# Moving one DMA sum five slots ahead, one load in front of two others, and two folds, in a fused attention + gated FFN kernel

## The chip, the cores and the metric

One NeuronCore of one Trainium2 chip runs the kernel. The metric is device time in microseconds (us), the median of several executions; smaller is better. A measurement of the kernel before and after takes the same inputs: four batches of 6016 rows with 256 columns, and weights 256 x 1536, 256 x 1536 and 1536 x 256.

## What is computed

```python
def _attn_ref(q, k, v, tau):                       # q, k, v: (4, 6016, 256)
    qn = q / (np.linalg.norm(q, axis=1, keepdims=True) + 1e-06)
    kn = k / (np.linalg.norm(k, axis=1, keepdims=True) + 1e-06)
    s = kn.transpose(0, 2, 1) @ qn / tau           # 256 x 256 per batch
    s = s - s.max(-1, keepdims=True)
    a = np.exp(s)
    a /= a.sum(-1, keepdims=True) + 1e-09
    return (v @ a).astype(np.float32)

def _moe_ref(x, w_gate, w_val, w_out):             # x: the result above, 24064 x 256
    gate = 1.0 / (1.0 + np.exp(-(x @ w_gate)))
    val = x @ w_val
    return (gate * val @ w_out).astype(np.float32)
```

The scores of a batch need all rows of its q and k; after that each row of v is on its own. Since the attention matrix `a` is only 256 x 256, the kernel multiplies it into the two input weights once per batch (the tiles `gh`, named G and H) and then applies G and H to v directly.

## The kernel before, in words

**Tiling.** The 6016 rows of a batch are 47 tiles of 128 rows. Four tiles make a *chunk* of 512 rows (the last has three), so a batch has 12 chunks, numbered 0 to 11. The 1536 hidden columns are 12 blocks of 128. One chunk runs through 12 *slots*, one for each block f: `glu(b, ci, f)` issues two matmuls into `ps_gate`, two into `ps_val`, a tanh on ScalarE (ACT) into `g_sb` (L656) and, on VectorE (DVE), the product into `hT` (L657). `ps_gate` and `ps_val` have two buffers each, so TensorE (PE) may be at most two slots ahead of ACT and DVE.

**Stages.** I call the 144 slots of batch b *stage b* (0 to 3). In the slots of a stage other work is put beside `glu`: the output matmuls `ps_o` of the chunk before, with DVE sums of `hT` (L679, `a_sum`: in slots 1, 3, 4, 5, 6 of a chunk for the second half of the previous chunk and in slots 7 to 11 for the first half of its own, none in slots 0 and 2); the evacuation of these results, which is two ACT copies (L733 into `m_sb`, L740 into `out_sb`) and four GpSimd (POOL) additions (L734, L735 on `m_sb`; L750, L751 on `out_sb`) for each pair of rows tiles; the store, from SyncE's (SP's) queue; and, in stages 0 to 2, the scores of the *next* batch.

**The next batch's scores.** The next batch's q and k come in six groups g0 to g5 of eight row tiles (the last of seven), q and k together in one tile `qk_sb`. Group g belongs to a first slot s0 = first + int(g * step), where first is 16 in stage 0 and 0 in the others, and step is (96 - first) / 6: 13.33 or 16 slots. In fixed slots after s0 each group gets: squares on ACT (L293, slots 0, 3, 6, 9) into `sq` tiles (two buffers); two accumulating DMAs of these into `acc` from POOL's queue (L304, slots 5 and 11); sums and differences of the halves of q and k, `qs0` to `qs4`, for a seven-product form of the score matmuls. `qs0`, `qs2`, `qs3`, `qs4` are DVE instructions (L328, L336, L341). `qs1`, the sum of q's two halves, is made by DMA: `score_sums` with m = 1 copies one half (L332, slot 1), and `score_sum_q` adds the other (L346, slot 6) with an accumulating DMA, which has to wait until the copy has landed. Both are issued from POOL's queue. `qs1` has two buffers. The score matmuls `ps_s` are spread from slot s0 + 3 (stage 0: s0 + 5) to the same point of the next group; the last two of the seven products read `qs1`.

**After the last group**, around slot 98 (s0 = 8 * FC + 2 in the code), `acc` is folded from eight tiles to one on DVE (L311: `acc_fold` with steps (4,), then (2, 1), for w = 1, k, and w = 0, q), `norms_mm` sums the columns, and the softmax and the next G and H follow.

**What sets the order.** `side_work(b)` writes a list by hand: `at(slot, fn, ...)` appends a call to the slot. Each engine works its instructions strictly in the order in which these calls issue them; inside a slot `glu` comes first, then the output matmuls, then the listed calls in the order of their appending. POOL therefore holds one sequence of additions and of DMA issues: `load_v` (L156), `load_qk` (L144, k then q; in stage 0 at max(9, s0 - 14), later at s0 - 24), `acc_add`, the two `qs1` DMAs. An instruction of POOL that waits holds back all that stand behind it. SP's queue holds the transposes of v (L621, `transpose_v`, into `vT`) and the stores.

`load_v` of chunk ci + 2 stands in slot 0 of chunk ci; only for (b, ci) = (0, 0) it stands in slot 10, behind the k and q load of g0 in slot 9. The loop over chunks stands first in `side_work`, so in equal slots `load_v` precedes `load_qk`.

Of the kernel before, what the change touches and what calls it, by code (L numbers as in the profile page):

```python
# [53 lines left out]
def kernel(  # L54
# [31 lines left out]
    FC = DFF // P  # L86
# [41 lines left out]
    def mm(out, lhsT, rhs, start, stop, **kw):  # L128
        nc.tensor.matmul(out, lhsT=lhsT, rhs=rhs, start=start, stop=stop, **kw)  # L129
# [30 lines left out]
    t0, nt = groups0[0]  # L160
# [39 lines left out]
    for f0, nf in pieces:  # L200
        if f0 + nf == DFF:
            load_v(0, 1)
        for w, src in enumerate((moe_w_gate, moe_w_val)):
            nc.gpsimd.dma_start(
                out=w_sb[w][f0 // FG][:, :, ds(f0 % FG, nf)],
# [6 lines left out]
    for n in range(FC // TPC):  # L212
        w_f32[n] = f32pool.tile([P, TPC, C], FP32, tag="f32", name="w_f32")
        nc.gpsimd.dma_start(
            out=w_f32[n], in_=moe_w_out.rearrange("(t p) c -> p t c", p=P)[:, n * TPC : (n + 1) * TPC, :]
# [16 lines left out]
    st = {}  # L232
# [82 lines left out]
    def score_sums(b, t0, m, halves):  # L315
        tl = qk[b, t0]
        s = st[b]
        if m == 0:
            s["sums"] = []
        out = qspool.tile([P, 2 * TPC, P], BF16, tag=f"qs{m}", name=f"qs{m}", bufs=1 + (m == 1))  # L320
        s["sums"].append(out)
        n = halves[0][1]
        lo, hi = (slice(h * TPC, h * TPC + n) for h in range(2))
        tt = nc.vector.tensor_tensor
        if m == 0:

            o = out.rearrange("p (t c) n -> p t c n", c=2).rearrange("p t c n -> p t (c n)")
            tt(out=o[:, :n], in0=tl[:, 1, hi, :], in1=tl[:, 1, lo, :], op=ALU.subtract)  # L328
        elif m == 1:

            o = out.rearrange("p (t c) n -> p t c n", c=2).rearrange("p t c n -> p t (c n)")
            nc.gpsimd.dma_start(out=o[:, :n], in_=tl[:, 0, lo, :])  # L332
        elif m == 2:

            o = out.rearrange("p (w t) n -> p w t n", w=2)
            tt(out=o[:, :, :n], in0=tl[:, :, lo, :P], in1=tl[:, :, hi, P:], op=ALU.add)  # L336
        else:

            w, op = ((0, ALU.subtract), (1, ALU.add))[m - 3]
            for u0, r in [(0, 2 * TPC)] if n == TPC else halves:  # L340
                tt(out=out[:, u0 : u0 + r], in0=tl[:, w, u0 : u0 + r, :P], in1=tl[:, w, u0 : u0 + r, P:], op=op)  # L341

    def score_sum_q(b, t0, halves):
        n = halves[0][1]
        o = st[b]["sums"][1].rearrange("p (t c) n -> p t c n", c=2).rearrange("p t c n -> p t (c n)")
        nc.gpsimd.dma_start(out=o[:, :n], in_=qk[b, t0][:, 0, TPC : TPC + n, :], accum_op=ALU.add)  # L346

    def score_work(b, t0, halves):
        tl, s = qk[b, t0], st[b]
        n = halves[0][1]  # L350
        first, last = t0 == 0, n < TPC
        work = []

        def raw(w, half, c):
            return lambda u: tl[:, w, half * TPC + u, ds(c * P, P)]

        def split(m, c):
            return lambda u: s_tile[m][:, 2 * u + c, :]

        def block(m, h):  # L360
            return lambda u: s_tile[m][:, h * TPC + u, :]

        s_tile = s["sums"]

        products = (
            (0, 0, raw(0, 0, 0), split(0, 1), None),
            (0, 1, raw(0, 1, 1), split(0, 0), (raw(0, 1, 1), raw(1, 1, 0))),
            (1, 0, block(2, 0), block(2, 1), (raw(0, 1, 1), raw(1, 1, 1))),
            (1, 1, block(3, 1), block(4, 1), (block(3, 1), block(4, 1))),
            (1, 2, block(3, 0), block(4, 0), None),  # L370
            (0, 2, split(1, 1), raw(1, 0, 0), None),
            (0, 3, split(1, 0), raw(1, 1, 1), (raw(0, 1, 0), raw(1, 1, 1))),
        )

        def go(i, bank, region, lhsT, rhs, u, end):
            if first and region == 0 and u == 0:
                pl, tag = ((pss, "s"), (psm, "m"))[bank]
                s["bank", bank] = pl.tile([P, 4, P], FP32, tag=tag, name=f"ps_s{bank}")
            mm(
                s["bank", bank][:, region, :],  # L380
                lhsT(u),
                rhs(u),
                start=(first and region == 0 and u == 0),
                stop=(last and end),
                skip_group_check=True,
            )

        for i, (bank, region, a, w, alone) in enumerate(products):
            us = [(a, w, u) for u in range(n)]
            if last and alone is not None:  # L390
                us += [(*alone, u) for u in range(n, TPC)]
            for e, (a1, w1, u) in enumerate(us):
                work.append((i, go, (i, bank, region, a1, w1, u, e == len(us) - 1)))
        return work
# [271 lines left out]
    sums = {}  # L666
# [169 lines left out]
    for g, (t0, nt) in enumerate(groups0):  # L836
# [11 lines left out]
        while adds:  # L848
            w, last_sq = adds.pop()
# [46 lines left out]
    def queue_scores(b, t0, halves):  # L896
        score_queue.extend(score_work(b, t0, halves))
# [7 lines left out]
    def side_work(b):  # L905


        side = {}

        def at(slot, fn, *a):  # L910
            side.setdefault(divmod(slot, FC), []).append((fn, a))

        for ci in range(NCH):
            nb, nci = (b, ci + 1) if ci + 1 < NCH else (b + 1, 0)
            lb, lci = (b, ci + 2) if ci + 2 < NCH else (b + 1, ci + 2 - NCH)
            if nb < B:
                at(ci * FC + 2, transpose_v, nb, nci)
            if lb < B:
                at(ci * FC + (10 if (b, ci) == (0, 0) else 0), load_v, lb, lci)
            if (b, ci) == (0, 0):  # L920
                for i in range(FC // TPC):
                    at(8, copy_w_out, i)
                for n, m in enumerate((1, 0, 3, 2, 4)):
                    for i in range(FC // TPC):
                        at(11 + 2 * n, sum_w_out, m, i)
        n = b + 1
        if n == B:
            return side
        first, last = (16 if b == 0 else 0), 8 * FC
        wide = [(t, min(2 * TPC, NT - t)) for t in range(0, NT, 2 * TPC)]  # L930
        step = (last - first) / len(wide)
        at(first - 1 if b == 0 else 0, acc_start, n)
        for g, (t0, nt) in enumerate(wide):
            s0 = first + int(g * step)
            halves = [(0, nt - TPC), (TPC, TPC)]
            if b == 0:
                at(max(FC - 3, s0 - 14), load_qk, n, t0, nt)
            elif s0 >= 24:
                at(s0 - 24, load_qk, n, t0, nt)
            for i in range(4):  # L940
                at(s0 + 3 * i, acc_square, n, t0, 1 - i // 2, halves, i % 2)
            for w in range(2):
                at(s0 + 11 - 6 * w, acc_add, n, t0, w, halves)
            late = 5 if b == 0 else 3
            for m, slot in enumerate((0, 1, 3, 6, 8 if b == 0 else 9)):
                at(s0 + slot, score_sums, n, t0, m, halves)
            at(s0 + 6, score_sum_q, n, t0, halves)
            end = first + int((g + 1) * step) + late
            at(s0 + late, queue_scores, n, t0, halves)
            for slot in range(s0 + late, end):  # L950
                at(slot, run_scores, s0 + late, end, slot)
        if n + 1 < B:
            for g, (t0, nt) in enumerate(wide[:2]):
                at(NCH * FC - 24 + 16 * g, load_qk, n + 1, t0, nt)
        s0 = 8 * FC + 2
        at(s0 - 3, acc_fold, n, 1, (4,))
        at(s0 - 2, acc_fold, n, 1, (2, 1))
        at(s0 + 1 if b == 0 else s0, acc_fold, n, 0, (4,))
        at(s0 + 2, acc_fold, n, 0, (2, 1))
        at(s0 + 5, score_out, n, 0)  # L960
        at(s0 + 6, norms_mm, n)
        at(s0 + 7, score_out, n, 1)
        at(s0 + 7, root_seed, n)
        at(s0 + 7, root_steps, n)
        at(s0 + 12, norms_inv, n)
        at(s0 + 12, spread_both, n)
        at(s0 + 14, read_row, n)
        at(s0 + 14, score_blocks, n)
        at(s0 + 22, scale_x, n, 0)
        at(s0 + 24, scale_x, n, 1)  # L970
        at(s0 + 25, exps, n, 0)
        at(s0 + 26, exps, n, 1)
        at(s0 + 28, all_sums, n)
        at(s0 + 28, gh_tiles, n)
        for i, piece in enumerate(gh_order):
            slot = s0 + 29 + 2 * i
            if slot < NCH * FC:
                at(slot, gh, n, piece, *((pss, "s"), (psm, "m"))[i % 2])
            else:
                spill.setdefault((n, *divmod(slot - NCH * FC, FC)), []).append((gh, (n, piece, psm, "m")))  # L980
        return side
# [73 lines left out]
```

## Time and profile before

| | |
|---|---|
| seven executions, median | 806.27 us |
| lowest and highest | 803.38 and 808.51 us |
| the profiled execution | 803.38 us, of which its span is 801.3 us |
| PE busy | 778.8 us of the span |
| granted PE clock over the span | 0.998 |
| DMA moved | 103.30 MB, 129 GB/s over the span |

The span runs from the first to the last instruction. Stage 0 begins at 37 us, after the first batch's scores; stages 1, 2 and 3 begin near 231, 423 and 615 us. A 512-column matmul pair starts 0.43 us before what follows it when nothing stalls, and a slot lasts 1.36 us where scores are made and 1.25 us where they are not.

How full the DMA engines are differs much between stages, and that is read from the page's second part, 40 slices of 20 us:

```profile
DMA  9999999962687999862578699877224223323302
GB/s 214 202 199 172 189 172 210 197 120 53 132 133 139 174 181 202 163 119 54 115 137 146 126 181 178 178 136 139 62 59 92 61 54 82 78 54 81 72 28 73
```

Each digit is the busy share of a slice in tenths. From 0 to 160 us, and around 260 to 320 and 460 to 520 us, the engines are nearly always busy; in stage 3 they are not. Where they are busy a transfer waits for those issued before it.

### The profile page before, as it was taken

What the parts mean: (1) busy time and instruction counts of PE and PEld (TensorE: products, weight loads), DVE (VectorE), ACT (ScalarE), POOL (GpSimd) and SP (SyncE); (2) the same over time, 40 slices, a digit from 0 to 9 for tenths busy, and PEclk for the clock granted to TensorE, in tenths of its full rate; (3) what the DMA queues carried; (4) which work ended last, traced back from release to release, by engine and by line L of the source; (5) the groups of instructions that cost most, each with busy time, mean ns of one, the idle gap of its engine ahead of it and who ended that gap; (6) DMA issues with size and microseconds to landing.
All of it is one profiled execution on the core that took longest, in us unless ns stands there. A gap on an engine that the chain in (4) does not pass through costs nothing.

```text
span 801.3 us, 18409 instructions
## 1 busy us (share of the span) xinstructions
PE 778.8 (97%) x6946; PEld 497.7 (62%) x6946; DVE 717.7 (90%) x1234; ACT 526.2 (66%) x893; POOL 416.8 (52%) x640
## 2 busy tenths in 40 slices
PE   3899999999999999999999999999999999999997
PEld 2556666666666666666666666666666566666666
DVE  5778999999979999999988999999998898998995
ACT  3766777766667667676667777666666566566563
POOL 3565667548443566565743564655744244444433
PEclk9999999999999999999999999999999999999999
DMA  9999999962687999862578699877224223323302
GB/s 214 202 199 172 189 172 210 197 120 53 132 133 139 174 181 202 163 119 54 115 137 146 126 181 178 178 136 139 62 59 92 61 54 82 78 54 81 72 28 73
DMA packets 84393, 103.30 MB, mean 129 GB/s; under 512 B 52736, under 2 KB 59136, under 8 KB 84304
## 3 DMA queue, kind: packets, MB, share of 16 engines
q0 software_dynamic: 27232, 63.98, 44.1%
q1 hardware_dynamic: 56496, 37.30, 21.5%
q8 instruction: 54, 0.88, 0.4%
q10 hardware_dynamic: 576, 0.85, 0.3%
q14 instruction: 35, 0.29, 0.1%
HBM read 79.04 MB, written 24.64 MB: 129 GB/s over the span
## 4 chain that ended last, share of the span: by engine, by line
PE 86%; DMA 9%; DVE 2%; POOL 1%; issue 1%; ACT 1%; POOLq 0%; DVEq 0%; ACTq 0%
PE ps_gate L129 28%; PE ps_val L129 28%; PE ps_o L129 26%; PE ps_s L129 3%; DMA qk_sb<-in_k_dram 3%; PE ps_gh L129 2%; DMA acc<-sq 2%; DMA w_f<-in_moe_w_out_dram 1%; DMA vT<-v_sb 1%; DMA v_sb<-in_v_dram 1%; DVE sums L679 1%; DMA w_gate<-in_moe_w_gate_dram 1%; DVE hT L657 1%; POOL qk_sb L144 0%; ACT sq L253 0%
## 5 line engine op out<-in xcount | busy, mean ns | idle before, releaser
L656 ACT ACTIVATE g_sb<-ps_gate 128x512 f32<-128x512 f32 (+1 forms) x576 | 338.0, 589 | 225.0 <-PE ps_gate L129 213.8
L657 DVE SCALAR_TENSOR_TENSOR hT<-g_sb,ps_val 128x512 bf16<-128x512 f32 (+1 forms) x576 | 385.9, 671 | 63.9 <-ACT g_sb L656 51.2
L129 PE MATMUL ps_gate<-vT,gh_G 128*128 128x512 bf16 (+1 forms) x1152 | 337.7, 375 | 1.0 <-DMA vT<-v_sb 1.0
L129 PE MATMUL ps_val<-vT,gh_H 128*128 128x512 bf16 (+1 forms) x1152 | 337.5, 375 | 0.8 <-DVE hT L657 0.8
L679 DVE TENSOR_TENSOR sums<-hT 128x768 bf16<-128x768 bf16 (+1 forms) x460 | 283.0, 615 | 0.0
L129 PEld LDWEIGHTS <-sums 128*128 128x128 bf16 x2670 | 183.0, 98 | 82.0
L129 PEld LDWEIGHTS <-gh_H 128*128 128x128 bf16 x1152 | 112.6, 98 | 132.2 <-issue 2.3
L750 POOL TENSOR_TENSOR out_sb<-out_sb,m_sb 128x256 f32<-128x256 f32 x89 | 78.8, 886 | 183.3 <-ACT out_sb L740 161.0
L129 PE MATMUL ps_o<-w_sums,sums 128*128 128x128 bf16 x1602 | 154.3, 219 | 0.0
L129 PEld LDWEIGHTS <-hT 128*128 128x128 bf16 x1200 | 88.3, 98 | 46.9
L734 POOL TENSOR_TENSOR m_sb<-m_sb 128x128 f32<-128x128 f32 x89 | 45.6, 513 | 125.8 <-ACT m_sb L733 125.6
L129 PEld LDWEIGHTS <-gh_G 128*128 128x128 bf16 x1152 | 90.6, 98 | 12.3 <-DMA vT<-v_sb 1.1
L129 PE MATMUL ps_o<-w_out_sb,sums 128*128 128x128 bf16 x1068 | 96.2, 219 | 0.0
L129 PE MATMUL ps_o<-w_sums,hT 128*128 128x128 bf16 x1068 | 95.5, 219 | 0.0
L751 POOL TENSOR_TENSOR out_sb<-out_sb 128x256 f32<-128x256 f32 x89 | 76.7, 862 | 7.0
L293 ACT ACTIVATE sq<-qk_sb 128x1024 bf16<-128x1024 bf16 (+1 forms) x60 | 61.9, 1031 | 0.4 <-DMA acc<-sq 0.4
L740 ACT COPY out_sb<-ps_o 128x512 f32<-128x512 f32 x89 | 52.2, 586 | 11.5 <-PE ps_o L129 9.1
L735 POOL TENSOR_TENSOR m_sb<-m_sb 128x128 f32<-128x128 f32 x89 | 55.1, 620 | 7.0
L733 ACT COPY m_sb<-ps_o 128x384 f32<-128x384 f32 x89 | 42.6, 479 | 3.3 <-PE ps_o L129 1.1
L129 PEld LDWEIGHTS <-qk_sb 128*128 128x128 bf16 x241 | 23.5, 105 | 21.3 <-issue 10.1
L129 PE MATMUL ps_s<-qk_sb 128*128 128x256 bf16 (+1 forms) x103 | 17.4, 318 | 15.7 <-DMA qk_sb<-in_k_dram 9.1
L304 POOL DMA_DIRECT2D acc<-sq x36 | 31.6, 926 | 0.8 <-issue 0.3
(99 smaller groups left out, 490.3 us busy)
## 6 DMA issues: line engine op xcount, KB each, us to landing
out_dram<-out_sb SPq DMA_DIRECT2D x43, 512.0 KB, 3.4
acc<-sq POOLq DMA_DIRECT2D x24, 512.0 KB, 6.0
v_sb<-in_v_dram POOLq DMA_DIRECT2D x44, 256.0 KB, 5.5
qk_sb<-in_q_dram POOLq DMA_DIRECT2D x19, 512.0 KB, 10.6
qk_sb<-in_k_dram POOLq DMA_DIRECT2D x19, 512.0 KB, 8.5
qs<-qk_sb POOLq DMA_DIRECT2D x30, 256.0 KB, 5.6
w_f<-in_moe_w_out_dram POOLq DMA_DIRECT2D x3, 512.0 KB, 10.0
acc<-sq POOLq DMA_DIRECT2D x6, 256.0 KB, 5.1
```

The costliest lines, as they stand in the source:

```text
L129: nc.tensor.matmul(out, lhsT=lhsT, rhs=rhs, start=start, stop=stop, **kw)
L293: nc.scalar.activation(out=s["sq", w][:, u0 : u0 + n, :], in_=src[:, u0 : u0 + n, :], func=ACT.Square)
L304: nc.gpsimd.dma_start(out=s["acc"][w][:, u0 : u0 + n, :], in_=s["sq", w][:, u0 : u0 + n, :], accum_op=ALU.add)
L656: nc.scalar.activation(out=g_sb[:, :n], in_=ps_gate[:, :n], func=ACT.Tanh, scale=0.5)
L657: nc.vector.scalar_tensor_tensor(out=hts[b, ci][:, f, :n], in0=g_sb[:, :n], scalar=1.0, in1=ps_val[:, :n], op0=ALU.add, op1=ALU.mult,)
L679: nc.vector.tensor_tensor(out=sums[b, ci, g][:, m, :, : half * P], in0=hT[:, f0 + k0 : f1 : 2, ds(r0 * half * P, half * P)], in1=hT[:, f0 ...
L733: nc.scalar.copy(m, states[p]["ps"][:, : 3 * P].rearrange("p (n c) -> p n c", c=P))
L734: nc.gpsimd.tensor_tensor(out=m[:, 1, :], in0=m[:, 1, :], in1=m[:, 2, :], op=ALU.add)
L735: nc.gpsimd.tensor_tensor(out=m[:, 2, :], in0=m[:, 1, :], in1=m[:, 0, :], op=ALU.add)
L740: nc.scalar.copy(o[:, p : p + half + 1 : half, :], states[p]["ps"].rearrange("p (t c) -> p t c", c=C),)
L750: add(out=ends, in0=ends, in1=states[p]["m"][:, 1:3, :], op=ALU.add)
L751: add(out=ends, in0=ends, in1=mids, op=ALU.subtract)
```

## The change

Four things are moved; no instruction is added or removed, and what is computed stays the same.

1. **q's sum of halves.** For g1 to g5 of every stage the copy moves from slot s0 + 1 to s0 - 4 and the accumulating DMA from s0 + 6 to s0 + 1. For g0 both stay. Since a group's `qs1` is now begun before the group itself, the tiles are kept by group (`s["sums", t0]`) in place of one list.
2. **v's third chunk.** In stage 0, `load_v(0, 2)` moves from slot 10 to slot 9 and so ahead of the k and q of g0.
3. **First slot.** In stage 0 `first` is 17 in place of 16, so step is 13.17 in place of 13.33; s0 goes from 16, 29, 42, 56, 69, 82 to 17, 30, 43, 56, 69, 82, and with it all that hangs on s0.
4. **Folds and norms of the first stage.** The folds of w = 1 go from slots 95 and 96 to 96 and 98, those of w = 0 from 99 and 100 to 101 and 102, and `norms_mm` from 104 to 105. In stages 1 and 2 they stay.

```diff
     def score_sums(b, t0, m, halves):
         tl = qk[b, t0]
         s = st[b]
-        if m == 0:
-            s["sums"] = []
         out = qspool.tile([P, 2 * TPC, P], BF16, tag=f"qs{m}", name=f"qs{m}", bufs=1 + (m == 1))
-        s["sums"].append(out)
+        s.setdefault(("sums", t0), {})[m] = out
...
     def score_sum_q(b, t0, halves):
         n = halves[0][1]
-        o = st[b]["sums"][1].rearrange("p (t c) n -> p t c n", c=2).rearrange("p t c n -> p t (c n)")
+        o = st[b]["sums", t0][1].rearrange("p (t c) n -> p t c n", c=2).rearrange("p t c n -> p t (c n)")
...
-        s_tile = s["sums"]
+        s_tile = s["sums", t0]
...
-                at(ci * FC + (10 if (b, ci) == (0, 0) else 0), load_v, lb, lci)
+                at(ci * FC + (9 if (b, ci) == (0, 0) else 0), load_v, lb, lci)
...
-        first, last = (16 if b == 0 else 0), 8 * FC
+        first, last = (17 if b == 0 else 0), 8 * FC
...
-            for m, slot in enumerate((0, 1, 3, 6, 8 if b == 0 else 9)):
+            for m, slot in ((0, 0), (2, 3), (3, 6), (4, 8 if b == 0 else 9)):
                 at(s0 + slot, score_sums, n, t0, m, halves)
-            at(s0 + 6, score_sum_q, n, t0, halves)
+            ahead = 0 if g == 0 else 5
+            at(s0 + 1 - ahead, score_sums, n, t0, 1, halves)
+            at(s0 + 6 - ahead, score_sum_q, n, t0, halves)
...
-        at(s0 - 3, acc_fold, n, 1, (4,))
-        at(s0 - 2, acc_fold, n, 1, (2, 1))
-        at(s0 + 1 if b == 0 else s0, acc_fold, n, 0, (4,))
-        at(s0 + 2, acc_fold, n, 0, (2, 1))
+        for w, n4, n21 in ((1, -2, 0), (0, 3, 4)) if b == 0 else ((1, -3, -2), (0, 0, 2)):
+            at(s0 + n4, acc_fold, n, w, (4,))
+            at(s0 + n21, acc_fold, n, w, (2, 1))
         at(s0 + 5, score_out, n, 0)
-        at(s0 + 6, norms_mm, n)
+        at(s0 + 7 if b == 0 else s0 + 6, norms_mm, n)
```

## The prediction

> **What bounds the kernel now.** I read the busy times first, then the waits of PE, then PE's starts around each wait, then the chain of waits behind them, and last POOL's timeline.
>
> ```profile
> PE 778.8 (97%) x6946; PEld 497.7 (62%) x6946; DVE 717.7 (90%) x1234; ACT 526.2 (66%) x893; POOL 416.8 (52%) x640
> PE ps_gate L129 <- DMA vT<-v_sb: 1.0, 1, 1.0
> PE ps_val L129 <- DVE hT L657: 0.8, 2, 0.5
> ```
>
> PE is the bound: its count and size of matmuls don't change, so only time in which it stands still can be won. After the start (to 37 us) the list of its waits holds next to nothing, so the whole prize is small, and it can be counted from PE's starts. A group's start to the next start is its price when nothing stalls: 0.43 us for a pair of 512 columns, 0.39 for seven of 128, 0.11 for two.
>
> ```profile
> 67.48 0.28 PE L129 MATMUL ps_s<-qs,qk_sb 128*128 128x128 bf16 x2
> 68.71 0.61 PE L129 MATMUL ps_gate<-vT,gh_G 128*128 128x512 bf16 x2 [0.96 <-DMA vT<-v_sb]
> ...
> 134.51 0.59 PE L129 MATMUL ps_gate<-vT,gh_G 128*128 128x512 bf16 x2
> 135.19 0.59 PE L129 MATMUL ps_val<-vT,gh_H 128*128 128x512 bf16 x2
> ...
> 176.93 0.59 PE L129 MATMUL ps_gate<-vT,gh_G 128*128 128x512 bf16 x2
> 178.05 0.59 PE L129 MATMUL ps_val<-vT,gh_H 128*128 128x512 bf16 x2 [0.52 <-DVE hT L657]
> ...
> 502.10 0.59 PE L129 MATMUL ps_gate<-vT,gh_G 128*128 128x512 bf16 x2
> 502.93 0.59 PE L129 MATMUL ps_val<-vT,gh_H 128*128 128x512 bf16 x2 [0.24 <-DVE hT L657]
> 503.36 0.55 PE L129 MATMUL ps_o<-w_sums,sums 128*128 128x128 bf16 x7
> 504.00 0.27 PE L129 MATMUL ps_s<-qs,qs 128*128 128x128 bf16 x2
> ```
>
> Four stalls: 68.71 - 67.48 - 0.11 = 1.12 us at 68.7; 135.19 - 134.51 - 0.43 = 0.25 at 135; 178.05 - 176.93 - 0.43 = 0.69 at 178; (0.83 - 0.43) + (0.64 - 0.39) = 0.65 at 502. Together 2.71 us, 0.34% of the time.
>
> **v's third chunk (68.7).** The chain of waits says why `vT` is late:
>
> ```profile
> 49.94 1.02 POOL qk_sb L144 x2
> 50.96 7.84 DMA v_sb<-in_v_dram
> 58.82 9.85 DMA vT<-v_sb
> 68.71 0.61 PE ps_gate L129 x2
> ```
>
> k and q (1 MB) are issued in front of v's 256 KB. After the change v is issued where k is now, 1.0 us earlier and with no megabyte in front. Such loads took 4.2 us (issued at 29.46) to 6.5 (issued at 53.55), so v lands near 54.2 to 56.5. The transposes that ran beside loads took 8.4 to 9.9 us, those in quiet stretches 3.1, so `vT` is there by 62.5 to 66.4; it is wanted at 67.6. Value: -1.1; bounds 0 (the transpose takes over 11 us) and -1.1. k and q are issued 0.6 us later and land some 1.3 us later behind v (256 KB at 200 GB/s); their readers (ACT's square at 58.0 for k, the `qs1` copy at 61.5 for q) move one slot, 1.3 us, with `first`. Cover: k landed 5.1 us after its issue at 49.9, so 3 us ahead of its first reader, q at 57.5, 4 us ahead. Cost 0. Without it ACT would hold `g_sb` by what is missing.
>
> **Folds of stage 0 (178).** The chain in front of 178.05 is DVE alone: product 0.6, L679 sums 0.5 to 0.6, fold 0.94, product, sums, fold 0.61. Before, w = 1's fold of 1.22 us stands in slot 95, beside sums; after, its parts stand in 96 and 98, which hold none. There DVE needs 0.68 + 1.22 = 1.90 and 0.68 + 0.74 = 1.42 against slots of 1.36. w = 0's folds stay beside sums (slots 101, 102 for 99, 100), where a slot needs 0.68 + 0.55 + 0.9 = 2.1 to 2.3, and where slots are 1.25 long. So the lag of DVE falls by the first part only. Value -0.45; bounds -0.69 (all gone) and +0.25 (slots 101 and 102 have less slack than 99 and 100). `norms_mm` a slot later still has three slots between its fold and itself; DVE's seed behind it starts after its own product, over 0.4 us after PE has passed. Cost 0.
>
> **q's sum, where it helps.** POOL's timeline at 500:
>
> ```profile
> 500.23 0.87 POOL L346 DMA_DIRECT2D qs<-qk_sb  x1 [2.41 <-DMA qs<-qk_sb]
> 500.81 1.05 POOL L750 TENSOR_TENSOR out_sb<-out_sb,m_sb 128x256 f32<-128x256 f32 x1
> ```
>
> POOL waits for its own copy (2.41 us); then its additions run in one burst, and a DVE sum beside them (500.55) takes 1.73 us, not 0.55. DVE is late, `ps_val` waits. At 135 it is the same after a wait of 5.25 us at 127.8: that copy, issued at 116.75 behind k and q of the next group (112.1), took 10.5 us. In stage 0 the copy now goes out at s0 - 4, ahead of that load at s0 - 1, so the waits of 5.25 and 2.65 us go; the one at 500 moves. Value: -0.25 - 0.65 = -0.90; lower bound that, upper 0.
>
> The Trainium skill ("SBUF — State Buffer", section "Who interferes with whom") says that a two-input VectorE operation and a GpSimd one that reads SBUF exclude each other for a whole instruction. By it one meeting would cost DVE up to 1.05 us, L750's length; the row lost 1.73 - 0.55 = 1.18.
>
> **q's sum, where it hurts.** In stages 1 and 2 the next k and q go out at s0 - 8 and a 512 KB `acc` sum at s0 - 5, just ahead of the copy at s0 - 4. These `acc` sums, issued at 269.97, 288.89, 461.73 and 480.65, took 10.3, 12.0, 11.3 and 13.8 us. The copy lands in turn, about 1 us behind. POOL reaches the accumulating DMA after the first pair's L751 (near 278, 294, 469.7, 485.5), so waits about 3.6, 8, 4.3 and 9.5 us: 25 us of new waits. Behind it stand the second pair's L750 and L751, the next v load (over a chunk early) and the next `acc` sum.
>
> ```profile
> 484.60 0.93 POOL L751 TENSOR_TENSOR out_sb<-out_sb 128x256 f32<-128x256 f32 x1
> 488.05 0.89 POOL L750 TENSOR_TENSOR out_sb<-out_sb,m_sb 128x256 f32<-128x256 f32 x1 [2.52 <-ACT out_sb L740]
> 495.19 0.48 ACT L733 COPY m_sb<-ps_o 128x384 f32<-128x384 f32 x1
> ```
>
> The copy at 495.19 reuses the `m_sb` buffer which L750 frees at 488.94: 6.25 us of cover. All six waits of before (19.8 us) cost PE 0.25 + 0.65, so 0.045 us per us; 25 us cost 1.15. Bounds: 0 (four of the six cost nothing) and 5 (if POOL goes on at 496 and issues 1.1 us, L750 ends at 498.0, ACT is held 2.8 us; at 303.4 likewise 1.1; 1.1 of DVE backlog behind). Value +1.15.
>
> The Trainium skill ("DMA: Bandwidth & Descriptors", section "Anatomy of one DMA — SWDGE (gpsimd) path") gives a POOL-queue DMA 2.0 us plus bytes at 436 GB/s: an estimate of 2.6 us for this copy, so no new wait in five slots, and a sum better by 1.15. The rows, 2.2 to 10.5 us, hold that only for an empty queue.
>
> **q's sum, the margin.** In the profiled execution the sum landed 1.0 us (133.4 for 134.4), 2.2 (150.3 for 152.5) and 1.7 us (485.5 for 487.2) ahead of its first matmul. This execution, 803.38, is the fastest of the seven; the median is 2.89 longer, and no row says where. Five slots (6.8 us) more would end every lateness here. Bounds 0 and -2.9; I take the middle, -1.45, since three sums of eighteen are that near.
>
> **Sum.** Profiled execution: -1.1 - 0.45 - 0.90 + 1.15 = -1.3, so 802.1 (span 800.0). Against the median the margin counts too: 806.27 - 1.3 - 1.45 = 803.5, -0.34%. A measurement here tells about 0.3% (2.4 us) from no change.
>
> **Rivals.**
> *Moved, not removed* (within 0.3%): the executions above 803.38 are long for another reason, the start to 37 us, which is DMA-bound and untouched. For it: DMA 9 tenths throughout the start. Then 806.27 - 1.3 = 805.0. It includes that the `vT` gain fails because k and q now run beside the transposes: 806.1.
> *POOL blocked* (slower): the accumulating DMA waits behind the `acc` sum longer than the `m_sb` cover; L733 holds ACT, so `g_sb`, so PE. It decides from 6.25 us between the first pair's L751 plus its gap and the landing. For it: 13.8 us of `acc`, 16.9 us of a transpose in the same stretch, DMA saturated. Against it: ACT is idle a third of the time, PE has two buffers, and only g3 of two stages exceeds the cover. At 8 us of price in place of 1.15, from two stages with g2 to g4 each: 806.27 - 2.45 + 8 = 811.8 without margin gain; at its threshold 808.7.
> *Not what it says*: the new sums' issue could still wait for a buffer. Against it: `qs1` has two, and PE leaves the older one eight slots or more ahead of s0. I give it nothing of its own.
>
> **How the numbers follow.** Forecast 0.45 (803.5, own range 800.5 to 803.9), moved 0.28 (803.9 to 808.7), POOL blocked 0.27 (808.7 to 812). Faster 0.45, same 0.28, slower 0.27. Range 800.3 to 810.5: it drops the longer half of the last case and a little below.
>
> **What would show it.** Right: no wait of `ps_gate` for `vT` at 68; L346's waits gone in stage 0 behind g1; no `ps_val` wait near 502. Wrong: ACT's L733 or L293 waiting for POOL or `acc` near 304 and 496; L346's waits above 45 us in total; a `ps_val` wait at 176 to 181 as long as before. If PE's stalls are gone and the time still stands, the margin was not it.

## The result, and the profile after

The changed kernel takes 812.53 us (median of 13 executions, 807.01 to 827.70) against 806.47 for the kernel before (34 executions). The ratio is 1.006, with a 95% interval of 1.0036 to 1.0084: it is slower by 0.6%, where a gain of 0.34% was forecast. (The medians take in every execution; the ratio leaves out the slow ones, four of the changed kernel's at 822 to 828 us and none of the kernel before's, so 812.53 / 806.47 is a little more than 1.006, and versions are compared by their ratios below.) The profiled execution took 810.05 us, its span 807.9 (before: 801.3).

The first view to read is again the list of waits, here the rows of PE and ACT that matter (us in total, times, longest). Most line numbers of the changed kernel are two lower than before: the tanh L656 is L654, the product L657 is L655, L740 is L738, L346 is L344; L293 and L304 stay.

```profile
PE ps_gate L129 <- ACT g_sb L654: 3.2, 2, 2.0
PE ps_o L129 <- ACT out_sb L738: 2.6, 1, 2.6
PE ps_val L129 <- DVE hT L655: 0.5, 2, 0.2
ACT sq L293 <- DMA acc<-sq: 9.1, 3, 3.6
```

`ps_gate` no longer waits for `vT`; it waits for ACT, and ACT for a DMA: the squares (L293) want a `sq` buffer, and that is free only when the accumulating sum that reads it has landed. Before, the last row was 0.4 us, once. PE's timeline shows what became of the four stalls of before and where the new ones are:

```profile
68.91 0.28 PE L129 MATMUL ps_s<-qs,qk_sb 128*128 128x128 bf16 x2
69.02 0.59 PE L129 MATMUL ps_gate<-vT,gh_G 128*128 128x512 bf16 x2
...
117.84 0.59 PE L129 MATMUL ps_gate<-vT,gh_G 128*128 128x512 bf16 x2 [2.00 <-ACT g_sb L654]
...
137.81 0.59 PE L129 MATMUL ps_gate<-vT,gh_G 128*128 128x512 bf16 x2 [1.24 <-ACT g_sb L654]
...
158.57 0.22 PE L129 MATMUL ps_o<-w_sums,hT 128*128 128x128 bf16 x1 [2.61 <-ACT out_sb L738]
...
185.55 0.59 PE L129 MATMUL ps_gate<-vT,gh_G 128*128 128x512 bf16 x2
186.37 0.59 PE L129 MATMUL ps_val<-vT,gh_H 128*128 128x512 bf16 x2 [0.23 <-DVE hT L655]
...
502.05 0.59 PE L129 MATMUL ps_gate<-vT,gh_G 128*128 128x512 bf16 x2
502.49 0.59 PE L129 MATMUL ps_val<-vT,gh_H 128*128 128x512 bf16 x2
```

The stall at 68 is gone (69.02 - 68.91 = 0.11, the price of two matmuls). The stall of the folds is 186.37 - 185.55 - 0.43 = 0.39 in place of 0.69, and the ones at 135 and 502 are gone. Three new ones stand in stage 0. The chain of waits names their cause:

```profile
101.37 0.72 POOL out_sb L748
...
102.17 0.93 POOL out_sb L749
103.10 0.52 POOL v_sb L156
103.62 12.61 DMA acc<-sq
...
122.51 13.69 DMA acc<-sq
...
141.13 15.57 DMA acc<-sq
```

Three sums of the squares, each of 512 KB (by their slots those of k, w = 1, of g2, g3 and g4), take 12.6, 13.7 and 15.6 us from issue to landing. In the kernel before, the same three took 6.6, 10.4 and 9.9. There the second held ACT for 0.4 us and the third landed at 149.02, 0.64 us before the square that needs its buffer, so the kernel before was already at the edge.

Stage by stage (each from its first `ps_gate` to that of the next stage, or to the end of the span), the loss lies in stage 0:

| us | to stage 0 | stage 0 | stage 1 | stage 2 | stage 3 | span |
|---|---|---|---|---|---|---|
| before | 36.8 | 193.8 | 191.8 | 192.5 | 186.5 | 801.3 |
| after | 36.8 | 199.6 | 192.8 | 192.3 | 186.5 | 807.9 |

Of the 6.6 us, 5.8 arise in stage 0. The gains forecast there are in it too (1.12 + 0.25 + 0.30 = 1.67), so something costs 7.5 us. The three large stalls and three of 0.3 to 0.4 us that follow them are 7.3 of that (between starts: 2.16 + 0.30 + 0.41 + 1.40 + 0.29 + 2.78).

### The profile page after: what moved, and what is told of

It reads as the page before. It is cut to its first block, busy times and chain, and to the rows that moved or that the text cites. A ratio compares the mean times of both kernels' runs of the same rounds, so it can differ in the third digit from the quotient of the medians.

```text
span 807.9 us, 18407 instructions
## 1 busy us (share of the span) xinstructions
PE 780.3 (97%) x6946; PEld 498.1 (62%) x6946; DVE 718.7 (89%) x1234; ACT 525.6 (65%) x893; POOL 414.9 (51%) x640
## 4 chain that ended last, share of the span: by engine, by line
PE 85%; DMA 9%; DVE 2%; issue 1%; ACT 1%; POOL 1%; ACTq 0%; POOLq 0%; DVEq 0%
PE ps_val L129 27%; PE ps_gate L129 27%; PE ps_o L129 25%; DMA acc<-sq 5%; DMA qk_sb<-in_k_dram 4%; PE ps_s L129 3%; PE ps_gh L129 3%; DVE hT L655 1%; DVE sums L677 1%; ACT g_sb L654 1%; DVE qs L339 0%; POOL out_sb L749 0%; POOL out_sb L748 0%; ACT out_sb L738 0%; POOL v_sb L156 0%
## 5 line engine op out<-in xcount | busy, mean ns | idle before, releaser
L654 ACT ACTIVATE g_sb<-ps_gate 128x512 f32<-128x512 f32 (+1 forms) x576 | 337.8, 589 | 222.7 <-PE ps_gate L129 211.3
L655 DVE SCALAR_TENSOR_TENSOR hT<-g_sb,ps_val 128x512 bf16<-128x512 f32 (+1 forms) x576 | 385.7, 671 | 69.6 <-ACT g_sb L654 56.4
L748 POOL TENSOR_TENSOR out_sb<-out_sb,m_sb 128x256 f32<-128x256 f32 x89 | 78.9, 887 | 175.3 <-ACT out_sb L738 153.2
L749 POOL TENSOR_TENSOR out_sb<-out_sb 128x256 f32<-128x256 f32 x89 | 75.6, 849 | 7.0
L293 ACT ACTIVATE sq<-qk_sb 128x1024 bf16<-128x1024 bf16 (+1 forms) x60 | 61.9, 1031 | 9.1 <-DMA acc<-sq 9.1
L738 ACT COPY out_sb<-ps_o 128x512 f32<-128x512 f32 x89 | 52.2, 586 | 11.0 <-PE ps_o L129 8.7
L344 POOL DMA_DIRECT2D qs<-qk_sb x18 | 15.9, 885 | 41.9 <-DMA qs<-qk_sb 35.6
```

The costliest lines, as they stand in the source:

```text
L293: nc.scalar.activation(out=s["sq", w][:, u0 : u0 + n, :], in_=src[:, u0 : u0 + n, :], func=ACT.Square)
L654: nc.scalar.activation(out=g_sb[:, :n], in_=ps_gate[:, :n], func=ACT.Tanh, scale=0.5)
L655: nc.vector.scalar_tensor_tensor(out=hts[b, ci][:, f, :n], in0=g_sb[:, :n], scalar=1.0, in1=ps_val[:, :n], op0=ALU.add, op1=ALU.mult,)
L738: nc.scalar.copy(o[:, p : p + half + 1 : half, :], states[p]["ps"].rearrange("p (t c) -> p t c", c=C),)
L748: add(out=ends, in0=ends, in1=states[p]["m"][:, 1:3, :], op=ALU.add)
L749: add(out=ends, in0=ends, in1=mids, op=ALU.subtract)
```

## The experiments

All runs in one table; each is explained below. The ratio is to the kernel before in the same job, that is, measured together with it on one chip. "Stage 0" is its length in the profiled execution, "L293" the time for which ACT's squares waited for the sums, in total.

| version | median us | ratio (95%) | stage 0 us | L293 us |
|---|---|---|---|---|
| after | 812.53 | 1.0060 (1.0036 to 1.0084) | 199.6 | 9.1 |
| e1: after, no q sum ahead | 807.20 | 1.0011 (0.9985 to 1.0036) | 196.6 | 3.0 |
| e2: before, with q sum ahead | 804.73 | 0.9996 (0.9973 to 1.0020) | 195.3 | 0 |
| e3: after, more buffers for squares | 806.45 | 0.9998 (0.9971 to 1.0025) | 196.5 | 0 |
| e4: after, ahead in stages 1, 2 alone | 808.70 | 1.0027 (1.0000 to 1.0054) | 199.0 | 5.4 |
| e5: after, first = 16 | 802.55 | 0.9945 (0.9919 to 0.9970) | 192.1 | 0 |
| e6: after, v's third chunk back | 816.86 | 1.0110 (1.0048 to 1.0173) | not used | not used |
| e7: after, sums of k's squares a slot earlier | 809.50 | 1.0024 (0.9999 to 1.0048) | 199.6 | 6.8 |
| e8: e5 with the buffers of e3 | 802.88 | 0.9949 (0.9927 to 0.9971) | 192.1 | 0 |
| e9: after, four sums back | 802.74 | 0.9964 (0.9945 to 0.9983) | 192.1 | 0 |
| e10: after, loads of k, q back | 813.11 | 1.0009 (0.9977 to 1.0040) | 201.5 | 6.2 |
| e11: e9 and e10 together | 802.54 | 0.9955 (0.9934 to 0.9976) | 192.9 | 0 |
| e12: e5, no q sum ahead | 803.66 | 0.9973 (0.9957 to 0.9989) | 192.6 | 0.8 |
| e13: after, two of the four sums back (q's) | 804.85 | 0.9994 (0.9971 to 1.0016) | 194.9 | 1.7 |
| e14: after, two of the four sums back (g1's) | 803.81 | 0.9985 (0.9950 to 1.0020) | 192.8 | 0 |
| e16: after, loads of k, q behind the transpose | 804.89 | 0.9985 (0.9958 to 1.0011) | 195.6 | 2.1 |

### Which part of the change is it? (e1, e2, e4, e5, e6)

Theory A at this point was that q's sum, begun ahead, puts 256 KB copies and sums in front of the sums of the squares. The other theories put the blame on another part, and each part was undone alone.

e1 (the changed kernel without the sum ahead) and e2 (the kernel before with it):

```diff
-            ahead = 0 if g == 0 else 5
+            ahead = 0
```

> The changed kernel without its first part: q's copy and sum stand at s0 + 1 and s0 + 6 again, the other three parts stay. Theory A (q's sum ahead puts its DMAs in front of the acc sums; these land late; ACT's squares wait for their buffer, PE for ACT): the three waits of L293 in stage 0 (9.1 us together after the change) fall under 1 us and the time is 803 to 806 us, below the kernel before. Theory B (first = 17 and v's third chunk moved ahead reorder POOL's queue, and they alone make the acc sums late): the waits stay above 6 us and the time stays at 809 to 813 us.

> The kernel before with q's sum ahead as the only edit. Theory A: L293 waits for acc in stage 0 for 6 us or more and the time is 810 to 815 us, since also the vT stall of 1.1 us at 68 stays. Theory B: L293 waits under 1.5 us, 804 to 807 us.

e2 settles that the sum ahead is not the cause by itself: with it and nothing else changed, ACT never waits for the sums, and the time stays as it was (0.9996). e1 is better than the changed kernel (1.0011 against 1.0060, intervals that meet without overlapping), but ACT still waits, 3.0 us, which is neither theory's figure, and the kernel isn't faster than before. The sum ahead adds to the load in a stretch that was made tight by something else.

e4 keeps it in stages 1 and 2 alone:

```diff
-            ahead = 0 if g == 0 else 5
+            ahead = 0 if g == 0 or b == 0 else 5
```

> The changed kernel with q's sum ahead in stages 1 and 2 alone; stage 0 has it at s0 + 1 and s0 + 6. Theory A, with the cost in stage 0: as without the first part, 803 to 806 us. The prediction's own rival (POOL blocked in stages 1 and 2): 808 to 812 us. POOL's waits of L344 in stages 1 and 2 (about 33 us after the change) should stay.

808.7 us is in the range that was set for the rival, but the profile puts the loss in stage 0: in stages 1 and 2 ACT waits neither for POOL nor for a DMA, in e4 or in any other version. In stage 0 e4 issues the same instructions as e1, yet its profiled stage 0 took 2.4 us more (a stall of 4.6 us at 120, against 2.0 in e1): with first = 17 the stage is so near the edge that one and the same order of instructions falls out differently. A difference of 2 us between two single profiles is therefore not evidence by itself.

e5 undoes `first`, e6 the order of v's third chunk:

```diff
-        first, last = (17 if b == 0 else 0), 8 * FC
+        first, last = (16 if b == 0 else 0), 8 * FC
```

> The changed kernel with first = 16 in stage 0 again, the other parts stay. Theory D (the shift to 17 puts g2's acc sum of k, slot 48, behind the v load of the same slot, and this one place begins the lateness): L293 waits for acc under 1.5 us, 802 to 805 us, and the vT stall at 68 is gone too. Theory E (PE comes earlier by what v's third chunk saves, while the crowded DMA queue of stage 0 does not, so the deadlines are missed whatever first is): the waits stay above 5 us and the time at 809 to 812 us.

```diff
-                at(ci * FC + (9 if (b, ci) == (0, 0) else 0), load_v, lb, lci)
+                at(ci * FC + (10 if (b, ci) == (0, 0) else 0), load_v, lb, lci)
```

> The changed kernel with v's third chunk behind k and q again (slot 10), first = 17 and the rest stay. Theory D: the acc waits stay, 809 to 813 us, with the vT stall of 1 to 2.4 us back. Theory E: PE is held 1 to 2.4 us at 68, so the later deadlines are met: L293 waits under 2 us, 805 to 808 us.

e5 takes one number back and is faster than both kernels, 0.55% below the one before. PE's waits after the start are then:

```profile
PE ps_val L129 <- DVE hT L655: 1.7, 3, 0.8
```

Undoing v's third chunk doesn't help: the ratio is 1.011, from three executions of 814.67 to 817.66 us, with an interval that overlaps that of the changed kernel, and theory E, which expected 805 to 808, is out. (Its profile fell on the longest execution, 828.93 us, so its stage times are not used; e2, which also has v in slot 10, shows the wait for `vT`, 2.3 us.) So the fault lies in `first`, which in the prediction has no term of its own. How much it costs depends on the sum ahead: with it 17 in place of 16 costs 1.15% (1.0060 against 0.9945), without it 0.38% (e1, 1.0011, against 0.9973 in e12 below, intervals that overlap).

### Is it the two `sq` buffers? (e3, e8)

The squares of k get the idle buffers of another pool, so that ACT need not wait for a sum that is late:

```diff
+    def more_squares():
+        t = f32pool.tile([P, TPC, C], FP32, tag="f32", name="sq_more")
+        return t.bitcast(BF16).rearrange("p t (h c) -> p (t h) c", c=C)
...
-                else wide_squares()
+                else wide_squares() if w == 0 else more_squares()
```

> The changed kernel with more buffers for the squares: those of k take the three 4 KB buffers that are idle after w_out's load, those of q keep two of their own; nothing else is moved. If the late acc sums cost time only by holding ACT's squares (theories A and B both say so), L293 waits for acc under 1 us and the time is 802 to 805 us, though the DMAs land as late as after the change. If the crowded DMA queue costs PE by another way (theory C: vT or q and k late), the time stays above 808 us.

> first = 16 and the further buffers for k's squares together, on the changed kernel. Theory D and E both: no acc wait is left; what remains is q's sum or vT landing late where the DMA queue is full. 802 to 805 us if that is rare; if it is above 806 us, the DMA queue of stage 0 is the bound whichever deadline is loosened.

L293's wait is gone in e3, and about half of the loss stays (0.9998, where first = 16 gives 0.9945): now other readers of late transfers stand in the list of PE's waits.

```profile
PE ps_s L129 <- DMA qs<-qk_sb: 2.1, 1, 2.1
PE ps_gate L129 <- DMA vT<-v_sb: 1.1, 1, 1.1
```

So the buffers are where lateness first shows, not where it arises. With first = 16 there is no lateness and the buffers bring nothing (e8: 0.9949, e5: 0.9945).

### Which steps of `first`? (e7, e9, e10, e11)

With 17, s0 of g0 to g2 is one slot later; int() makes g3 to g5 fall in the same slots. What moves is ACT's, DVE's and PE's work of three groups, q's copies and sums of halves for them, the k and q loads of g1 and g2, and four sums of squares: k's (w = 1) and q's (w = 0) of g1 and g2. g0 has none.

e7 moves the sums of k's squares of all groups in stage 0 one slot earlier:

```diff
-                at(s0 + 11 - 6 * w, acc_add, n, t0, w, halves)
+                at(s0 + 11 - (7 if b == 0 else 6) * w, acc_add, n, t0, w, halves)
```

> The changed kernel with the acc sums of k of stage 0 one slot earlier (s0 + 4). On POOL this exchanges one pair only: g2's acc sum and the v load of slot 48. Theory D: the first ACT wait (2.8 us near 113) goes and what follows it shrinks, 803 to 807 us. Theory E, or a cause elsewhere in the queue: 809 to 812 us.

The first wait is gone and a longer one comes one group later (4.8 us). A miss as a cure (1.0024, above the 803 to 807 us of theory D), but the place of the sums moves the waits. e9 moves exactly the four sums that `first` had moved, e10 the loads, e11 both:

```diff
-                at(s0 + 11 - 6 * w, acc_add, n, t0, w, halves)
+                at(s0 + 11 - 6 * w - (b == 0 and g < 3), acc_add, n, t0, w, halves)
```

> The version with first=16 (802.55 us) and the changed kernel (812.53 us) differ in stage 0 alone, and there only by one slot for groups g0, g1 and g2 (steps for g3 to g5 fall in the same slots). Here the changed kernel keeps first=17, and only the accumulating sums of g1 and g2 go back to their slots of first=16 (four DMAs, each one slot earlier). Theory F1 (the sums of the squares themselves come too late): 802 to 805 us, L293 waits under 1 us in stage 0. Theory F2 (it is the k and q load of g2, which fell behind POOL's additions on m_sb: issued at 77.3 us, with first=16 at 74.6): 808 to 812 us, L293 still waits 5 to 9 us and the transposes of slots 42 and 54 still take over 15 us. Theory G (the squares, sums and products on ScalarE, VectorE and TensorE in their new slots): 808 to 812 us too.

```diff
-                at(max(FC - 3, s0 - 14), load_qk, n, t0, nt)
+                at(max(FC - 3, s0 - 14 - (g < 3)), load_qk, n, t0, nt)
```

> First=17, and only the k and q loads of g1 and g2 go back to their slots of first=16 (15 and 28). F2: 802 to 805 us, L293 waits under 1 us in stage 0, transposes of slots 42 and 54 at 9 to 12 us. F1 and G: 808 to 812 us, L293 waits 5 to 9 us.

> First=17, and both the accumulating sums and the k and q loads of g0 to g2 in their slots of first=16: the order on POOL is then that of the version with first=16, and only ScalarE's squares, VectorE's sums and TensorE's score products stand one slot later. F1, F2 or both together: 802 to 804 us, as with first=16. G: 808 us or more, with L293 still waiting for the sums.

This is the clearest of the results: F1 holds. Four DMA issues, each one slot earlier, take the ratio from 1.0060 to 0.9964 (7.7 us of 806.5), and stage 0 from 199.6 to 192.1 us. The loads alone don't cure it: in e10's profile ACT waits 6.2 us, and its executions scatter from 802.43 to 826.11 us, so that 1.0009 tells little. ACT, DVE and PE in their new slots do no harm (e11 is like e5). POOL's timeline shows how one slot becomes 4.3 us. The changed kernel:

```profile
81.67 0.72 POOL L749 TENSOR_TENSOR out_sb<-out_sb 128x256 f32<-128x256 f32 x1
84.91 0.73 POOL L748 TENSOR_TENSOR out_sb<-out_sb,m_sb 128x256 f32<-128x256 f32 x1 [2.51 <-ACT out_sb L738]
85.72 0.93 POOL L749 TENSOR_TENSOR out_sb<-out_sb 128x256 f32<-128x256 f32 x1
86.59 0.87 POOL L304 DMA_DIRECT2D acc<-sq  x1
...
93.98 0.88 POOL L304 DMA_DIRECT2D acc<-sq  x1
94.56 0.86 POOL L144 DMA_DIRECT2D qk_sb<-in_k_dram  x1
```

and e9:

```profile
81.56 0.73 POOL L749 TENSOR_TENSOR out_sb<-out_sb 128x256 f32<-128x256 f32 x1
82.31 0.88 POOL L304 DMA_DIRECT2D acc<-sq  x1
84.81 0.71 POOL L748 TENSOR_TENSOR out_sb<-out_sb,m_sb 128x256 f32<-128x256 f32 x1 [1.62 <-ACT out_sb L738]
...
91.71 0.90 POOL L304 DMA_DIRECT2D acc<-sq  x1
...
93.87 0.58 POOL L144 DMA_DIRECT2D qk_sb<-in_k_dram  x1
```

The sum has slipped behind a pair of additions that wait 2.51 us for ACT, and the next one comes to stand right in front of the k load. POOL's busy time is the same in both (414.9 and 414.8 us); only the times of the issues differ. The queues in the 2 us from 96 to 98 show what follows. The changed kernel (packets, MB, share of 16 engines) has no row for q1:

```profile
q0 software_dynamic: 78, 0.32, 113.8%
```

and e9:

```profile
q1 hardware_dynamic: 1024, 0.26, 85.1%
q0 software_dynamic: 33, 0.08, 21.3%
```

q0 holds what POOL issues, q1 what SP issues; a packet's whole time counts where it starts, so a share can pass 100%. In e9 the transpose of slot 42 moves all of its 1024 packets (256 KB) in these 2 us and takes 7.5 us from issue to landing. In the changed kernel it was issued at 94.79, and none of its packets moves while q0 fills the engines. From 98 to 106 q1 gets 23 to 109 packets per 2 us, from 106 to 108 it gets 661, and the transpose lands after 17.9 us. From 100 to 102 us the changed kernel has

```profile
q0 software_dynamic: 109, 0.39, 97.4%
q1 hardware_dynamic: 109, 0.03, 10.0%
```

and the next two stretches of 2 us have 96 and 95, 103 and 106 packets. While both queues have work they get the same number of packets. But a packet of the transpose is 256 B (1024 of them make 256 KB) and one of q0 is 3.6 KB on average here, so the transpose goes through at the pace of one small packet for each large one. (The next transpose takes 13.3 us in e9 and 18.0 in the changed kernel, the third 5.9 and 12.7: e9 recovers, the changed kernel doesn't.) The stretch from 80 to 160 us (length, busy times, clock, DMA share, GB/s) never recovers in the changed kernel,

```profile
80.00:100.00 20.00, 20.00 (x191) 13.02 (x189) 19.01 (x32) 15.16 (x25) 12.10 (x17) 1.00 0.93 173
100.00:120.00 20.00, 17.87 (x172) 11.59 (x170) 16.70 (x28) 12.60 (x21) 10.55 (x15) 1.00 1.12 197
120.00:140.00 20.00, 18.39 (x173) 11.79 (x172) 17.36 (x30) 14.05 (x23) 12.71 (x19) 1.00 1.11 174
140.00:160.00 20.00, 17.39 (x168) 11.36 (x167) 16.09 (x28) 12.25 (x22) 8.44 (x13) 1.00 1.16 177
```

where e9 has

```profile
80.00:100.00 20.00, 20.00 (x191) 12.98 (x189) 19.02 (x32) 15.15 (x25) 12.16 (x17) 1.00 1.01 203
100.00:120.00 20.00, 20.00 (x197) 13.28 (x195) 19.39 (x32) 14.69 (x24) 12.66 (x18) 1.00 1.02 197
120.00:140.00 20.00, 20.00 (x191) 13.04 (x190) 19.17 (x31) 14.79 (x24) 13.49 (x20) 1.00 1.10 200
140.00:160.00 20.00, 20.00 (x194) 13.14 (x192) 18.79 (x34) 14.79 (x25) 11.71 (x17) 1.00 0.90 184
```

The first row matters most: before anything stalls, the changed kernel moves 173 GB/s at a share of 0.93 where e9 moves 203. 30 GB/s over 20 us are 0.6 MB, about one sum of 512 KB, which is carried into a stretch where the engines are always busy. In this profile later transfers stay late up to 160 us, after which the share falls (0.75 from 160 to 180 us). Whether the bytes put off or the order of the transfers does this, the next runs ask.

### One sum or all, and load or order? (e13, e14, e16)

e13 puts back only q's two sums, e14 only g1's two; e16 leaves all sums as changed and issues the k and q loads of g3 and g4 three slots later, behind the transposes:

```diff
-                at(s0 + 11 - 6 * w, acc_add, n, t0, w, halves)
+                at(s0 + 11 - 6 * w - (b == 0 and g < 3 and w == 0), acc_add, n, t0, w, halves)
```

> Of the four sums that e9 put back, only q's (w=0) of g1 and g2 stand one slot earlier. Theory O (what counts is that no sum is issued between the transpose of slot 42 and the k and q load, and the transpose comes first): transpose of slot 42 at 6 to 11 us, 802 to 806 us. Theory S (what counts is k's sum of g1, which in e9 filled the DMA engines at 84 to 88 us, share 1.06 against 0.72 in the changed kernel): 808 to 813 us, with the share at 84 to 88 us at 0.7.

```diff
-                at(s0 + 11 - 6 * w, acc_add, n, t0, w, halves)
+                at(s0 + 11 - 6 * w - (b == 0 and g == 1), acc_add, n, t0, w, halves)
```

> Both sums of g1 one slot earlier, those of g2 as in the changed kernel. Theories O and S both: the stretch to 103 us runs as in e9 (transpose of slot 42 at 7 to 8 us). If the first backlog is the cause and all later ones only carry it on: 802 to 804 us. If each group has to keep its own place: the wait of L293 comes back near 130 us, 806 to 810 us.

```diff
-                at(max(FC - 3, s0 - 14), load_qk, n, t0, nt)
+                at(max(FC - 3, s0 - 14 + 3 * (g in (3, 4))), load_qk, n, t0, nt)
```

> All sums as in the changed kernel; the k and q loads of g3 and g4 in stage 0 three slots later, behind q's sum ahead and behind the transpose. Theory O (the transpose has to share the DMA engines with the 1 MB of k and q): transposes of slots 42 and 54 at 4 to 9 us, no wait of L293 over 1 us, 802 to 806 us. Theory S (DMA work put off into a full stretch): the loads are put off still further, so no better than the changed kernel: 808 us or more, L293 waits of 3 us and more.

The three ratios (0.9994, 0.9985, 0.9985) all lie below that of the changed kernel, with intervals that don't meet its own, and can't be told from each other or from e9's.

e14: the two sums of g1 are enough in the profiled execution (L293 waits 0, stage 0 192.8 us), and its median is 803.81. There the sums of g2 need not go back: it is the first backlog that counts, the later waits carry it on. But three of its ten executions took 812.95 to 816.80 us, so it isn't shown to be enough each time. e13 gives back 0.66 of the 0.96% with q's sums alone, although the transpose was issued 0.9 us after the k load and took 14.3 us, against what O expected of it; one wait of 1.7 us is left. In e13 k's sum of g1 is as late as in the changed kernel (issued at 87.72), and in e7 it was issued as early as in e9 (82.25) while stage 0 stayed at 199.6. So the 4.3 us of that sum are the plainest shift on POOL's timeline, but by these profiles not the larger part of the loss: putting back q's sums, the first of which stood right in front of the k load, gave more. (e7 moves the k sums of g3 to g5 too; k's two sums alone were not run.) e16 goes against S: the loads are put off further still, and from 80 to 100 us it moves 173 GB/s like the changed kernel, and yet it is better by 0.75%, with the transposes of slots 42 and 54 at 6.6 and 7.4 us. From 96 to 104 us it had:

```profile
qk_sb<-in_k_dram POOLq DMA_DIRECT2D x1, 512.0 KB, 6.7
qk_sb<-in_q_dram POOLq DMA_DIRECT2D x1, 512.0 KB, 9.7
qs<-qk_sb POOLq DMA_DIRECT2D x1, 256.0 KB, 4.1
vT<-v_sb SPq DMA_TRANSPOSE x1, 6.6
```

One wait of L293 of 2.1 us stays in e16, because the first sum is still late (11.9 us to landing). So both seem true in part: the sum put off is late by itself, and the transpose that meets the megabyte of k and q turns one lateness into a chain of them. What share of the 0.96% each part has remains open; e13 and e16 leave 0.3 and 0.2% of it.

### What the parts that were meant to help are worth (e12)

> First=16 and q's sum of halves not begun ahead: what is left of the change is v's third chunk ahead of k and q and the moved folds and norms. If these carry the gain of the version with first=16 (802.55, ratio 0.9945): 802.5 to 804 us and ratio 0.995 to 0.997, the wait for the transpose near 70 us gone, the fold's stall at 0.4 us. If q's sum ahead carries it, about as before: 805 to 807 us, with PE stalls of 0.5 to 1 us for L346's late sums (135 and 502 us in the kernel before).

Its edit is that of e1 and of e5 together. v's third chunk and the folds alone give 0.27% (0.9973). With the sum ahead it is 0.55% (e5, another job) or 0.45% and 0.36% (e11 and e9, the same job, intervals overlapping): by these medians the sum ahead is worth 0.1 to 0.3%, and no run here tells that surely from nothing.

## Why the prediction was wrong, step by step

**The step that failed.** In the passage on v's third chunk the prediction says that k's and q's readers "move one slot, 1.3 us, with `first`" and writes "Cost 0". It used the shift of `first` as cover only and gave it no term, although four accumulating DMAs hang on s0. It had the queue rule in its other passages (an instruction of POOL holds back those behind it) and didn't apply it to L304: g1's sum for k moved past a waiting pair L748, L749 and was issued 4.3 us later, not 1.36, and g1's sum for q came to stand right in front of the k load (93.98 and 94.56). This step is worth 0.96%, 7.7 us (1.0060 against 0.9964 in e9, where these four sums alone go back). A second term stood at nothing: for stage 0 the prediction gave the sum ahead a gain and no cost, while with first = 17 taking it back in all stages gains 0.49% (e1, 1.0011).

**The rival on the losing side had the right chain and the wrong place.** "POOL blocked" had the accumulating sum late, ACT held, then `g_sb`, then PE, and named ACT's L293 waiting for `acc` as the sign. It looked near 304 and 496 only, because it took the sum ahead for the cause. There nothing of the kind happened: in no version's profile does ACT wait for POOL or for a DMA in stages 1 and 2. What would have shown stage 0 as the place was in the profile of before: the 0.4 us of L293, and a landing that was 0.64 us ahead of need.

**v's third chunk: right.** Gain 1.12 for a forecast of 1.1. It was issued at 49.3 and landed at 53.4, and the transpose took 8.0 us.

**Folds: nearly right.** 0.30 for 0.45. The stall is 0.39 us in the profiles with the folds moved of e1, e4, e5, e8, e9, e11, e12 and e14 as well, and 0.69 and 0.68 in the two without, that of before and e2.

**q's sum where it helps: right in this profile.** The stalls at 135 and 502 (0.90 us) are gone, and in e12, without the sum ahead, 0.34 us remain near 135 and 0.81 near 504. But e11, with it, has 0.72 us near 502, so one profile doesn't settle it.

**q's sum where it hurts: the waits of POOL right, their price not shown.** L344's waits (L346 before) rose to 35.6 us in ten, in stages 1 and 2 as forecast for g2 to g4 (up to 6.4 us). POOL's timeline near 500 in the changed kernel:

```profile
502.41 0.87 POOL L344 DMA_DIRECT2D qs<-qk_sb  x1 [5.45 <-DMA qs<-qk_sb]
502.99 1.16 POOL L732 TENSOR_TENSOR m_sb<-m_sb 128x128 f32<-128x128 f32 x1
```

5.45 us of wait, and PE shows no stall beside it (502.49 above): what stands behind is needed later. Three stalls of 0.25, 0.60 and 0.51 us in stages 1 and 2 (at 318, 340 and 532) sum to 1.35, near the +1.15; but they wait for DVE's L339, and in e9, with 27 us of the same waits, there is none. That POOL's waits cost nothing in e9 is measured; that they cause the three is not. Stages 1 and 2 together last 383.4 to 386.3 us in the profiles with the sum ahead there and 384.1 to 384.4 in the three without (before, e1, e12), so a cost of some 1 us is lost in the scatter, and the rival's 8 us is excluded.

The Trainium skill ("DMA: Bandwidth & Descriptors", section "Issuing engines are not separate DMA queues") says that transfers from SP, ACT and POOL run on the same 16 engines and interleave. The rows above agree: 109 packets of each queue from 100 to 102 us in the changed kernel, and in e9 1024 of the transpose in 2 us where POOL's transfers leave room. Even in packets is not even in bytes: 0.03 MB against 0.39.

**The margin of the late sums (-1.45): not shown as such.** e2 has the sum ahead alone, and its ratio is 0.9996 (0.9973 to 1.0020). The forecast for the whole, -0.34%, is near what the change gives without the four delayed sums (-0.36% in e9, -0.45% in e11); as its largest part is this margin, which no run shows, the agreement is luck.

## What to carry to other kernels

A number that shifts a group's first slot shifts all DMA issues that hang on it, and each has to be followed through its queue: one slot became 4.3 us because the issue slipped behind an addition that waits for another engine. In a stretch where the DMA engines are always busy, what is issued late may not be made up until the stretch ends (here to 160 us; e13 made it up by 140), so look for issues moved out of the last part with idle engines, and for transfers that land less than 1 us ahead of need. When several small moves come together, undo one at a time: here v's chunk and the folds were sound (e12), q's sum ahead was not told from nothing, and the version with `first` taken back or its four sums put back (e5, 0.9945; or e9, 0.9964) beats both kernels.

## What the runs showed that was not expected

A long stall of PE costs more than its length. In e10 PE stood still for 5.38 us up to 122.37. The windows of e10 (the third number from the end is the granted clock):

```profile
118.00:120.00 2.00, 0.00 (x0) 0.00 (x0) 0.00 (x0) 0.00 (x0) 0.00 (x0) 1.00 1.13 281
120.00:122.00 2.00, 0.00 (x0) 0.00 (x0) 0.00 (x0) 1.23 (x2) 0.28 (x1) 0.77 1.03 206
122.00:124.00 2.00, 1.63 (x4) 0.56 (x4) 1.65 (x3) 1.39 (x3) 0.61 (x1) 0.50 1.08 211
...
126.00:128.00 2.00, 2.00 (x14) 1.45 (x13) 0.93 (x2) 1.04 (x2) 1.92 (x3) 0.52 1.05 185
128.00:130.00 2.00, 2.00 (x18) 1.18 (x16) 0.84 (x2) 0.70 (x2) 1.05 (x2) 1.00 1.26 190
```

From 121.1 to 127.9 us the clock is at half, over 5 us of it while PE works again: a pair of 512 columns, started at 123.17, then starts 0.86 us before what follows it, not 0.43. The same followed stalls of 4.6 us (e4, 3.4 us at half) and 3.5 us (e7, 6.8 us), but not those of 2.2 and 2.8 us in the changed kernel's profile. The Trainium skill ("TensorE: Matmul & The Clock Gate", section "What's actually happening") has the clock halve after an idle window of about 3.4 us and return after a busy one; these three cases agree, with 3.4 to 6.8 us at half. e6's profile does not: there 3.4 us at half followed stalls of 2.3 and 2.8 us as well (ended at 69.81 and 177.45), so a stall shorter than that window can halve the clock, and these runs give no limit below which it doesn't.

The transpose was the other surprise: 256 KB from SBUF to SBUF took 3.1 us with the engines free and 18.0 beside loads of k and q, 1 MB, on the other queue.
